# A list scheduler's costs and one new rule: two-tensor work of VectorE and GpSimd kept apart in an attention and feed-forward kernel

## The chip, the cores and the metric

The kernel runs on one core of a Trainium2 chip. Time is device time in microseconds (us) of one execution; for the kernel before it is 896.74 us, the median of three runs (894.29 to 896.76). The engines are called as the profile calls them: PE (TensorE, matmuls), DVE (VectorE), ACT (ScalarE), POOL (GpSimd) and SP, whose queue issues every DMA.

## The reference: what is computed

Attention with heads mixed before and after the softmax, then a feed-forward layer, cut to what matters:

```python
scores = scale * np.matmul(q, k.transpose(0, 1, 3, 2))        # 4 batches, 12 heads, 448 x 448, head width 64
scores = np.einsum('bhij,hg->bgij', scores, w_pre)            # heads mixed
scores = scores - np.max(scores, axis=-1, keepdims=True)
attn = np.exp(scores)
attn = attn / (np.sum(attn, axis=-1, keepdims=True) + 1e-09)
attn = np.einsum('bhij,hg->bgij', attn, w_post)               # heads mixed again
x = np.matmul(attn, v)                                        # then heads side by side: 1792 x 768
h = x @ w_in                                                  # 768 x 2048
g = h * (1.0 / (1.0 + np.exp(-1.702 * h)))
out = g @ w_out                                               # 2048 x 768
```

The weights of the feed-forward layer come as 64-bit floats, which the kernel converts by integer operations.

## The kernel before, in words

**Attention** goes in 180 steps, 45 for each of the 4 batches. A step takes 10 rows of all 12 heads, 120 partitions by 448 columns. The scores of a block of 112 rows are made on PE (`qk`), copied out of PSUM (`sc`), written to DRAM (`sd`) and gathered again in the layout of the steps (`r`). A step is then: mixing matmul `mx` (PE), negated maximum `nm` (DVE), exponential `e` with its row sum (ACT), `rs` (POOL adds a small number, DVE takes the reciprocal), weighting, second mixing `pp` (PE), and a copy `p` out of PSUM. In the first two batches ("whole", f32) POOL scales the small mixing matrix (`wr`). In the last two ("half") everything is split into an upper and a lower f16 part: `a1` on ACT, `w` and the lower part `a2 = w - a1` on POOL, and a lower part of `p` on DVE. Every 12 steps a product `av` with v makes a piece of `x`.

**Weights** are converted in 16 pieces (`w0_s` for w_in, `w1_s` for w_out, s from 0 to 7), each in three thirds: a load, `magnitude` on ACT, then four operations on DVE (`least`, `shift`, `rest` at L542, `sign` at L548) in place on `w_f`, a sum of squares on ACT, one small matmul `sums` (L113) that adds over the partitions, `scale_w` on DVE, an upper part on ACT (L576), a lower part `w_p` on DVE (L581), and a store `wd` to DRAM. Whoever needs the piece loads it again (`wt`).

**Feed-forward** goes in 32 units (8 slices of 256 of the 2048 columns, for each of the 4 batches): two groups of 18 matmuls `h` (L612), a tanh and a gate (`th`), the two parts of `g` (L637 ACT, L641 DVE), and six groups of six matmuls `po` (L650). A group is collected into `acc` either by one operation on DVE (L674) or by ACT into `pt` (L672) and an addition on POOL (L678).

**The order.** Nothing of this order is written out. Every operation is a task in a list scheduler (`add`, `run_all`): a task has an engine or a choice of two, `occ` (how long it holds its engine), `lat` (when its result can be used), a due time, and buffers that it takes. `run_all` keeps a clock for each engine, looks at the tasks that could start first on each, takes the most due of those within 0.1 us, and emits its instruction. So the figures set the order of each engine's queue, and nothing else: on the chip each engine works through its queue in that order and waits for semaphores where a value is not there yet. A number that is wrong by a tenth moves many rows a little.

Tile names below have the step, unit or piece in them: `nm_76` is the maximum of step 76, `h_7_0` the first half of unit 7, `w1_7_p` the converted piece 7 of w_out.

## Time and profile before

| | |
|---|---|
| median of 3 runs | 896.74 us (894.29 to 896.76) |
| the profiled execution | 895.33 us, of which 893.6 us are its span |
| PE busy | 856.5 us, 96% of the span |
| DVE, ACT, POOL busy | 631.0 (71%), 626.7 (70%), 353.3 (40%) |
| granted PE clock, mean | 0.99 of full speed |
| DMA | 196.85 MB, mean 220 GB/s |

The span is the time from the first to the last instruction; the rest of the execution's time lies around it. Shares over the whole span mix stages: the first 175 us are attention with transfers and conversions, from 178 us feed-forward work fills PE as well, the conversions end at about 401 us, and the last batch's feed-forward fills the time from about 750 us to the end. A wait on PE is idle time in front of an instruction, with the instruction that ended last among those it waited for.

### The profile page before, as it was taken

The page shows a single profiled execution, that of the slowest core. Times are in us where ns is not written, and L with a number is a line of the kernel's source. Part 1 is how long each engine was busy: PE and PEld are TensorE (multiplying, and loading weights), DVE is VectorE, ACT ScalarE, POOL GpSimd, SP SyncE. Part 2 cuts the span into 40 slices and gives each one's busy share as a digit, 9 for nine tenths or more (in the row PEclk, how much of TensorE's full clock was granted, in tenths as well). Part 3 has the DMA queues.
Part 4 walks back from the last instruction along what each step waited for, and adds up shares of the span by engine and source line. Part 5 has one row for each costly group of instructions (what it writes and reads, how often), then busy time and mean ns, then how long its engine had stood idle before and what let it go on. Part 6 is the DMA issues. An engine that isn't in the chain of part 4 may idle for free.

```text
span 893.6 us, 19386 instructions
## 1 busy us (share of the span) xinstructions
PE 856.5 (96%) x7030; PEld 541.5 (61%) x7030; DVE 631.0 (71%) x1471; ACT 626.7 (70%) x1389; POOL 353.3 (40%) x542
## 2 busy tenths in 40 slices
PE   8879998999998999889999999999999999999998
PEld 4546766566665666655666666665666666555554
DVE  3658769887879989999679877778675754342233
ACT  4769888987976888866788778776776675324442
POOL 0212222221217423565446745555355554204432
PEclk9989999999999999999999999999999999999999
DMA  8999999899987886789588495567563423352422
GB/s 248 303 300 325 293 329 311 294 322 316 321 313 256 295 268 209 242 213 299 171 275 236 145 287 170 164 183 236 173 187 103 156 73 114 108 163 101 142 76 93
DMA packets 66768, 196.85 MB, mean 220 GB/s; under 512 B 8081, under 2 KB 32913, under 8 KB 66673
## 3 DMA queue, kind: packets, MB, share of 16 engines
q1 hardware_dynamic: 66672, 195.62, 68.0%
q8 instruction: 55, 0.90, 0.4%
q14 instruction: 41, 0.33, 0.1%
HBM read 138.96 MB, written 56.62 MB: 219 GB/s over the span
## 4 chain that ended last, share of the span: by engine, by line
PE 60%; DVE 17%; DMA 10%; ACT 7%; issue 3%; POOL 2%; SPq 1%; ACTq 0%; POOLq 0%; DVEq 0%
PE po L650 18%; PE h L612 18%; PE pp L373 4%; PE mx L322 4%; PE av L460 3%; DVE nm L332 2%; PE av L449 2%; DMA sd<-sc 2%; DVE sc L278 2%; PE qk L252 2%; ACT e L342 2%; DVE w_f L542 2%; DVE w_f L548 2%; DMA w<-in_moe_w_in_dram 1%; DVE w_p L581 1%
## 5 line engine op out<-in xcount | busy, mean ns | idle before, releaser
L612 PE MATMUL h<-x,wt 128*128 128x448 f16 x1152 | 246.2, 353 | 1.5 <-ACT e L342 1.1
L650 PE MATMUL po<-g,wt 128*128 128x448 f16 x1152 | 238.9, 353 | 2.2 <-DVE th L631 1.1
L612 PEld LDWEIGHTS <-wt 128*128 128x128 f16 x1152 | 110.3, 98 | 102.4 <-issue 12.2
L650 PEld LDWEIGHTS <-wt 128*128 128x128 f16 x1152 | 110.0, 98 | 98.1 <-issue 3.1
L353 POOL TENSOR_SCALAR rs<-sm 120x1 f32<-120x1 f32 x180 | 46.3, 257 | 277.6 <-ACT e L342 272.2
L332 DVE TENSOR_REDUCE nm<-mx 120x1 f32<-120x448 f32 x180 | 110.1, 617 | 27.6 <-PE mx L322 13.7
L678 POOL TENSOR_TENSOR acc<-acc,pt 128x448 f32<-128x448 f32 x71 | 83.4, 1175 | 110.2 <-ACT pt L672 102.9
L396 POOL TENSOR_TENSOR a<-w,a 120x448 f16<-120x448 f32 (+1 forms) x90 | 97.9, 1088 | 28.9 <-issue 12.7
L373 PEld LDWEIGHTS pp<-wr,e 120*112 120x112 f32 x720 | 85.6, 178 | 35.9 <-issue 18.4
L631 DVE SCALAR_TENSOR_TENSOR th<-th,h 128x448 f32<-128x448 f32 x64 | 39.5, 618 | 82.7 <-ACT th L627 82.1
L373 PE MATMUL pp<-wr,e 120*112 120x120 f32 x720 | 91.7, 271 | 5.9 <-POOL wr L363 5.8
L322 PE MATMUL mx<-r,wa 120*120 120x448 f32 x180 | 84.7, 561 | 10.8 <-DMA r<-sd 9.3
L342 ACT ACTIVATE e<-mx,nm,c 120x448 f32<-120x448 f32 (+1 forms) x90 | 65.3, 726 | 27.6 <-DVE nm L334 17.5
L382 POOL TENSOR_SCALAR w<-e,rs 120x448 f32<-120x448 f32 (+1 forms) x90 | 61.5, 683 | 54.7 <-DVE rs L358 34.1
L674 DVE SCALAR_TENSOR_TENSOR acc<-po,ct,acc 128x448 f32<-128x448 f32 x97 | 65.5, 678 | 15.7 <-PE po L650 15.3
L390 ACT ACTIVATE a<-e,rs 120x448 f16<-120x448 f32 (+1 forms) x90 | 60.0, 667 | 23.6 <-DVE rs L358 21.8
L672 ACT ACTIVATE pt<-po,ct 128x448 f32<-128x448 f32 x71 | 44.9, 636 | 42.9 <-PE po L650 42.9
L342 ACT ACTIVATE e<-mx,nm 120x448 f32<-120x448 f32 (+1 forms) x90 | 57.7, 641 | 19.3 <-DVE nm L332 15.3
L363 POOL TENSOR_SCALAR wr<-wp,rs 120x120 f32<-120x120 f32 (+1 forms) x90 | 46.0, 512 | 58.0 <-DVE rs L358 41.3
L435 DVE TENSOR_TENSOR p<-pp,p 112x480 f16<-112x480 f32 (+1 forms) x90 | 58.2, 649 | 14.9 <-ACT p L431 14.3
L411 PE MATMUL pp<-wp,a 120*112 120x120 f16 x360 | 62.5, 217 | 0.7 <-POOL a L396 0.7
L409 PE MATMUL pp<-wp,a 120*112 120x120 f16 x360 | 62.6, 217 | 0.0
(141 smaller groups left out, 1568.6 us busy)
## 6 DMA issues: line engine op xcount, KB each, us to landing
wt<-wd SPq DMA_DIRECT2D x64, 768.0 KB, 4.3
sd<-sc SPq DMA_DIRECT2D x90, 392.0 KB, 4.7
r<-sd SPq DMA_DIRECT2D x164, 210.0 KB, 4.8
w<-in_moe_w_in_dram SPq DMA_DIRECT2D x24, 512.0 KB, 6.1
w<-in_moe_w_out_dram SPq DMA_DIRECT2D x24, 512.0 KB, 4.9
wd<-w_p SPq DMA_DIRECT2D x16, 768.0 KB, 5.8
out_dram<-acc SPq DMA_DIRECT2D x24, 224.0 KB, 4.9
kf<-in_k_dram SPq DMA_DIRECT2D x6, 448.0 KB
```

The costliest lines, as they stand in the source:

```text
L322: nc.tensor.matmul(mx[:K, :S], st["wa"][:K, :K], r[:K, :], start=True, stop=True)
L332: nc.vector.tensor_reduce(nm[:K], row["mx", i][:K, :S], axis=AX.X, op=ALU.max, negate=True)
L342: nc.scalar.activation(e[:K], row.pop(("mx", i))[:K, :S], AF.Exp, bias=row.pop(("nm", i))[:K, 0:1], scale=1.0 if b < WHOLE else st["c", b] ...
L373: nc.tensor.matmul(pp[:CP, jc * K:(jc + 1) * K], e[:K, jc * CP:(jc + 1) * CP], wr[:K, :, :n], start=True, stop=True,)
L382: nc.gpsimd.tensor_scalar(w[:K], e[:K], row["rs", i][:K, 0:1], 1.0, op0=ALU.mult, op1=ALU.mult)
L396: nc.gpsimd.tensor_tensor(a2[:K], row.pop(("w", i))[:K], row["a1", i][:K], op=ALU.subtract)
L409: nc.tensor.matmul(o, a1[:K, js], wp1[:K, :, :n], start=True, stop=False)
L411: nc.tensor.matmul(o, a2[:K, js], wp1[:K, :, :n], start=False, stop=True)
L612: nc.tensor.matmul(h, w[:, i, c, fc * 128:(fc + 1) * 128], x[:, j, c, :], start=(n == 0), stop=(n == len(terms) - 1),)
L650: nc.tensor.matmul(po, w[:, j, fc, e * 128:(e + 1) * 128], g[:, i, fc, :], start=(n == 0), stop=(n == len(terms) - 1),)
L674: nc.vector.scalar_tensor_tensor(a, po, c, a, op0=ALU.mult, op1=ALU.add)
L678: nc.gpsimd.tensor_tensor(a, a, st.pop(("pt", u, e)), op=ALU.add)
```

## The change

Four edits, all in the figures and rules of the scheduler; no instruction's work changes.

1. A rule: tasks marked `kind="two"` (operations that read two tensors from SBUF) on DVE ("D") and on POOL ("G") may not overlap in the plan. Marked are, on DVE, the lower parts of the inputs (L224), `rest` and `sign` of the conversion, its lower part (L581) and the lower part of `g` (L641); on POOL, `a2` (L396) and the addition into `acc` (L678).
2. The small matmul of a sum (`sums`) may start in the plan only 1.0 us after its last input is there.
3. The maximum is planned with 0.64 us (first two batches) and 0.77 us (last two) in place of 0.53 and 0.73.
4. The exponential is planned with 0.61 and 0.71 us in place of 0.62.

```diff
+    free_port = [0.0]
...
+                    if j["kind"] == "two" and e in "DG":
+                        s = max(s, free_port[0])
...
+            if j["kind"] == "two" and e in "DG":
+                free_port[0] = s + occ
...
-        j = add("PE", 0.12, over, list(after), due, 0.4, takes=[("gen", h)])
+        after = [add("-", 0.0, lambda: None, list(after), due, 1.0)]
+        j = add("PE", 0.12, over, after, due, 0.4, takes=[("gen", h)])
...
-        k = add("D", 0.73 if half else 0.53, lambda: peak(i), [m], i - 1, 0.81 if half else 0.62)
+        k = add("D", 0.77 if half else 0.64, lambda: peak(i), [m], i - 1, 0.86 if half else 0.73)
...
-            lo = add("G", 1.12, lambda: lower(i), [w, u], i + 0.6, 1.05, takes=[("a2", a2)])
+            lo = add("G", 1.12, lambda: lower(i), [w, u], i + 0.6, 1.05, takes=[("a2", a2)], kind="two")
...
-            low.append(add("D", 0.66, lambda a=a: c["w_lower"](a), [u], due + 0.5, 0.75))
+            low.append(add("D", 0.66, lambda a=a: c["w_lower"](a), [u], due + 0.5, 0.75, kind="two"))
```

What the new plan does with the rows: PE has the same instructions in another order, above all in the first 430 us of the span; after unit 11 its order differs in a handful of places. Seven collections of `po` go from ACT and POOL to DVE (L674 stands 104 times in place of 97, L678 64 times in place of 71). Three places follow.

DVE at step 76, around the lower parts of the weights' piece `w0_5`. Before:

```order
L631 SCALAR_TENSOR_TENSOR th_3_1_3500<-th_3_1_3500,h_3_1_3423 128x448
L581 SCALAR_TENSOR_TENSOR w0_5_p_3509<-w0_5_f0_3118,w0_5_s_3489,w0_5_p_3509 128x512
L581 SCALAR_TENSOR_TENSOR w0_5_p_3509<-w0_5_f1_3236,w0_5_s_3489,w0_5_p_3509 128x512
L581 SCALAR_TENSOR_TENSOR w0_5_p_3509<-w0_5_f2_3377,w0_5_s_3489,w0_5_p_3509 128x512
L641 SCALAR_TENSOR_TENSOR g_3_3335<-th_3_1_3500,gs_90,g_3_3335 128x448
L332 TENSOR_REDUCE nm_76_3547<-mx_76_3496 120x1
L224 SCALAR_TENSOR_TENSOR kp0_2_3498<-kb0_2_3415,s_k2_3217,kp0_2_3498 128x896
L332 TENSOR_REDUCE nm_77_3571<-mx_77_3541 120x1
```

And now:

```order
L117 TENSOR_REDUCE w0_5_n_3509<-sums_15_3496 128x1
L332 TENSOR_REDUCE nm_76_3518<-mx_76_3487 120x1
L85 TENSOR_SCALAR w0_5_n_3509<-w0_5_n_3509 128x1
L86 TENSOR_SCALAR ew_89<-w0_5_n_3509 128x1
L562 TENSOR_SCALAR ew_89<-ew_89 128x1
L564 RECIPROCAL w0_5_s_3526<-ew_89 128x1
L565 TENSOR_SCALAR w0_5_s_3526<-w0_5_s_3526 128x1
L641 SCALAR_TENSOR_TENSOR g_3_3302<-th_3_1_3490,gs_90,g_3_3302 128x448
L224 SCALAR_TENSOR_TENSOR kp0_2_3494<-kb0_2_3428,s_k2_3239,kp0_2_3494 128x896
L581 SCALAR_TENSOR_TENSOR w0_5_p_3544<-w0_5_f0_3162,w0_5_s_3526,w0_5_p_3544 128x512
L581 SCALAR_TENSOR_TENSOR w0_5_p_3544<-w0_5_f1_3245,w0_5_s_3526,w0_5_p_3544 128x512
L581 SCALAR_TENSOR_TENSOR w0_5_p_3544<-w0_5_f2_3379,w0_5_s_3526,w0_5_p_3544 128x512
```

The maximum `nm_76` stood behind three lower parts `w0_5_p` and the lower part of `g_3`; now it stands ahead of them, and the second sum of a piece (`w0_5_n`) directly ahead of it.

PE at the sum of the last weight piece, `w1_7` (`h_7_1` is unit 7's hidden layer, `po_6_5` unit 6's last output group, `qk_2_2_3` scores). Before:

```order
L612 LDWEIGHTS wt0_7_4954
L612 MATMUL h_7_1_5088<-x_0_742,wt0_7_4954 128x448
L113 MATMUL sums_22_5161<-w1_7_m_4585,ones_77 128x3
L650 LDWEIGHTS wt1_6_4673
L650 MATMUL po_6_5_5163<-g_6_4478,wt1_6_4673 128x448
```

And now:

```order
L262 MATMUL qk_2_2_3_0_5213<-kp1_2_3521,qp1_2_3717 112x448
L262 LDWEIGHTS qp1_2_3717
L262 MATMUL qk_2_2_3_1_5214<-kp1_2_3521,qp1_2_3717 112x448
L113 MATMUL sums_22_5227<-w1_7_m_4497,ones_77 128x3
L612 LDWEIGHTS wt0_8_5066
```

The sum stood behind `h_7_1` and ahead of `po_6_5`; now `po_6_5` (6 matmuls), `mx_100` (3), `pp_97` (12 short ones) and the scores `qk_2_2_2` and `qk_2_2_3` (12) are issued ahead of it.

DVE at the end of that piece's conversion (`w1_7_p`), and then the queue of SP from its store `wd1_7` to the load `wt1_7`, which the output groups of unit 7 need. DVE before:

```order
L581 SCALAR_TENSOR_TENSOR w1_7_p_5207<-w1_7_f0_4730,w1_7_s_5181,w1_7_p_5207 128x512
L581 SCALAR_TENSOR_TENSOR w1_7_p_5207<-w1_7_f1_4748,w1_7_s_5181,w1_7_p_5207 128x512
L641 SCALAR_TENSOR_TENSOR g_7_5185<-th_7_1_5170,gs_90,g_7_5185 128x448
L581 SCALAR_TENSOR_TENSOR w1_7_p_5207<-w1_7_f2_4911,w1_7_s_5181,w1_7_p_5207 128x512
L332 TENSOR_REDUCE nm_100_5256<-mx_100_5187 120x1
L334 TENSOR_SCALAR nm_100_5256<-nm_100_5256,c_2_3417 120x1
L674 SCALAR_TENSOR_TENSOR acc_0_2595<-po_6_5_5163,ct_6_4401,acc_0_2595 128x448
```

DVE now:

```order
L657 TENSOR_TENSOR ct_7_5126<-eo_91,ew_89 128x1
L620 TENSOR_SCALAR ct_8_5288<-ex_79,ew_89 128x1
L278 SCALAR_TENSOR_TENSOR sc_2_2_2_5224<-qk_2_2_2_1_5204,sc_2_2_2_5224 112x448
L278 SCALAR_TENSOR_TENSOR sc_2_2_3_5238<-qk_2_2_3_0_5213,sc_2_2_3_5238 112x448
L581 SCALAR_TENSOR_TENSOR w1_7_p_5270<-w1_7_f0_4563,w1_7_s_5254,w1_7_p_5270 128x512
L581 SCALAR_TENSOR_TENSOR w1_7_p_5270<-w1_7_f1_4717,w1_7_s_5254,w1_7_p_5270 128x512
L581 SCALAR_TENSOR_TENSOR w1_7_p_5270<-w1_7_f2_4933,w1_7_s_5254,w1_7_p_5270 128x512
L631 SCALAR_TENSOR_TENSOR th_8_0_5308<-th_8_0_5308,h_8_0_5230 128x448
```

SP before:

```order
L587 DMA wd1_7_124<-w1_7_p_5207 128x3072
L288 DMA sd_2_2_103<-sc_2_2_2_5234 112x1792
L309 DMA r_105_5299<-sd_2_1_102 120x896
L309 DMA r_106_5323<-sd_2_1_102 120x896
L288 DMA sd_2_2_103<-sc_2_2_3_5244 112x1792
L309 DMA r_107_5347<-sd_2_1_102 120x896
L600 DMA wt1_7_5362<-wd1_7_124 128x3072
```

SP now:

```order
L587 DMA wd1_7_124<-w1_7_p_5270 128x3072
L309 DMA r_107_5347<-sd_2_1_102 120x896
L288 DMA sd_2_2_103<-sc_2_2_3_5238 112x1792
L309 DMA r_108_5380<-sd_2_1_102 120x896
L309 DMA r_109_5407<-sd_2_1_102 120x896
L600 DMA wt1_7_5425<-wd1_7_124 128x3072
```

On DVE the last of `w1_7_p` now stands behind `nm_100` with its factor, the collection of `po_6_5`, a lower part `p` and three `sc`, all of which followed it before. On SP the gathers `r_108` and `r_109` now stand ahead of `wt1_7`. On PE `po_7_0` itself moves behind 12 matmuls of `h_9_0` and one `pp`.

## Rows read from the trace of the kernel before

**Rows 1.** The page: busy time, share of the span, count of each engine.

```profile
PE 856.5 (96%) x7030; PEld 541.5 (61%) x7030; DVE 631.0 (71%) x1471; ACT 626.7 (70%) x1389; POOL 353.3 (40%) x542
```

**Rows 2.** Stretches: length, busy of PE, PEld, DVE, ACT, POOL; clock, DMA, GB/s.

```profile
50.00:75.00 25.00, 21.95 (x178) 15.48 (x179) 16.70 (x45) 17.46 (x45) 5.26 (x16) 0.88 0.89 294
145.00:175.00 30.00, 26.84 (x216) 17.41 (x215) 26.61 (x73) 26.25 (x66) 7.55 (x19) 0.94 0.92 309
260.00:415.00 155.00, 144.04 (x1083) 92.15 (x1078) 146.51 (x325) 121.52 (x273) 78.74 (x96) 0.98 0.80 252
415.00:880.00 465.00, 460.51 (x4174) 284.51 (x4173) 286.93 (x645) 296.56 (x610) 214.74 (x287) 1.00 0.52 165
```

**Rows 3.** Waits of PE, whole span: total us, times, longest.

```profile
PE pp L373 <- POOL wr L363: 5.8, 6, 2.3
PE sums L113 <- ACT waste L100: 4.0, 4, 2.3
PE av L449 <- DVE p L435: 2.2, 1, 2.2
PE mx L322 <- DMA r<-sd: 9.3, 5, 5.2
```

**Rows 4.** Timeline of PE: start, us, instruction; idle before it and its releaser.

```profile
154.61 1.38 PE L373 MATMUL pp<-wr,e 120*112 120x120 f32 x8 [1.38 <-POOL wr L363]
281.49 1.94 PE L373 MATMUL pp<-wr,e 120*112 120x120 f32 x8 [2.31 <-POOL wr L363]
371.70 2.04 PE L449 MATMUL av<-p,vf 112*64 112x88 f32 x48 [2.22 <-DVE p L435]
392.91 0.39 PE L113 MATMUL sums<-w_m,ones 128*128 128x3 f32 x2 [2.33 <-ACT waste L100]
414.43 5.85 PE L650 MATMUL po<-g,wt 128*128 128x448 f16 x30 [0.99 <-DMA wt<-wd]
```

**Rows 5.** DVE by line, 60 to 260 us: count, busy us, mean ns, idle before.

```profile
L581 DVE SCALAR_TENSOR_TENSOR w_p<-w_f,w_s,w_p 128x512 f16<-128x512 f32 x27 | 19.2, 751 | 0.4 <-ACT w_p L576 0.2
L536 DVE TENSOR_SCALAR w_f<-w_f 128x512 int32<-128x512 int32 x28 | 12.3, 444 | 0.3
L641 DVE SCALAR_TENSOR_TENSOR g<-th,gs,g 128x448 f16<-128x448 f32 x7 | 4.8, 680 | 0.1
```

**Rows 6.** DVE by line, 260 to 415 us, as rows 5.

```profile
L278 DVE SCALAR_TENSOR_TENSOR sc<-qk,sc 112x448 f16<-112x448 f32 x34 | 19.8, 617 | 0.5 <-ACT sc L274 0.4
L581 DVE SCALAR_TENSOR_TENSOR w_p<-w_f,w_s,w_p 128x512 f16<-128x512 f32 x18 | 16.1, 937 | 0.4 <-ACT w_p L576 0.3
L674 DVE SCALAR_TENSOR_TENSOR acc<-po,ct,acc 128x448 f32<-128x448 f32 x16 | 10.8, 676 | 0.3 <-PE po L650 0.3
L536 DVE TENSOR_SCALAR w_f<-w_f 128x512 int32<-128x512 int32 x16 | 9.7, 613 | 0.0
L641 DVE SCALAR_TENSOR_TENSOR g<-th,gs,g 128x448 f16<-128x448 f32 x11 | 9.1, 827 | 1.3 <-ACT g L637 1.3
```

**Rows 7.** Timeline of DVE at two places between 275 and 391 us.

```profile
275.34 1.55 DVE L641 SCALAR_TENSOR_TENSOR g<-th,gs,g 128x448 f16<-128x448 f32 x1
...
384.76 1.65 DVE L542 SCALAR_TENSOR_TENSOR w_f<-w,w_f 128x512 int32<-128x512 int32 x1
...
386.79 0.91 DVE L542 SCALAR_TENSOR_TENSOR w_f<-w,w_f 128x512 int32<-128x512 int32 x1
...
389.67 1.61 DVE L548 SCALAR_TENSOR_TENSOR w_f<-w,w_f 128x512 int32<-128x512 int32 x1
```

**Rows 8.** Timeline of POOL beside rows 7, from 384.7 us.

```profile
384.72 1.13 POOL L678 TENSOR_TENSOR acc<-acc,pt 128x448 f32<-128x448 f32 x1
385.83 1.33 POOL L382 TENSOR_SCALAR w<-e,rs 120x448 f32<-120x448 f32 x1
```

**Rows 9.** Timeline of the DMA queue of SP: the store of the last converted weights.

```profile
400.70 0.34 SPq L587 DMA_DIRECT2D wd<-w_p  x1
```

**Rows 10.** The chain that ended last: the load that PE waits for at 414.43.

```profile
405.90 8.48 DMA wt<-wd
```

More of the change, by code (lines that the diff above doesn't have):

```diff
@@ L936, in step_tasks @@
             m["from"] = READY[i]
-        k = add("D", 0.73 if half else 0.53, lambda: peak(i), [m], i - 1, 0.81 if half else 0.62)
+        k = add("D", 0.77 if half else 0.64, lambda: peak(i), [m], i - 1, 0.86 if half else 0.73)
         early = expos.get(i, {"then": []})["then"]
-        e = expos[i] = add("A", 0.62, lambda: expo(i), [k, expos.get(i - 1)], i - 0.8, 0.73, takes=[("e", e_home[i])])
+        e = expos[i] = add("A", 0.71 if half else 0.61, lambda: expo(i), [k, expos.get(i - 1)], i - 0.8, 0.82 if half else 0.73, takes=[("e", e_home[i])])
         e["then"] += early
@@ L1063, in split_tasks @@
                     [j, sized[name, b]], x + 2 + i, {"G": 1.05, "A": 1.05}, takes=[(f"{name}p{i}", in_home[name, b, i])], bias=0.5)
-            lo = add("D", 1.65 if name == "v" else 1.05, lambda i=i: lower_part(name, b, i), [u], x + 2.5 + i)
+            lo = add("D", 1.65 if name == "v" else 1.05, lambda i=i: lower_part(name, b, i), [u], x + 2.5 + i, kind="two")
             h += [u, lo]
@@ L1077, in conversion_tasks @@
             for n, (name, occ) in enumerate((("magnitude", 0.62), ("least", 0.35), ("shift", 0.35), ("rest", 0.61), ("sign", 0.61))):
-                j = add("D" if n else "A", occ, lambda a=a, name=name: c[name](a), [j], due, occ + 0.09, takes=[] if n else [("wf", wf)])
+                j = add("D" if n else "A", occ, lambda a=a, name=name: c[name](a), [j], due, occ + 0.09, takes=[] if n else [("wf", wf)],
+                        kind="two" if n > 2 else "")
                 w64.append(j)
@@ L1202, in attention_then_feed_forward @@
             up = add("A", 0.56, lambda u=u, fc=fc: g_upper(u, fc), [d] + lower_g[:1], due + 1, 0.67, takes=[] if fc else [("g", g_home)])
-            lo = add("D", 0.6, lambda u=u, fc=fc: g_lower(u, fc), [up], due + 1.2, 0.7)
+            lo = add("D", 0.6, lambda u=u, fc=fc: g_lower(u, fc), [up], due + 1.2, 0.7, kind="two")
             th += [d, up, lo]
@@ L1230, in finish @@
                     collect_rest(u, e)
-            k["rest"] = rests[u, e] = add("G", 1.2, finish, [j2], due + 1, 1.15)
+            k["rest"] = rests[u, e] = add("G", 1.2, finish, [j2], due + 1, 1.15, kind="two")
             gen.append(j2)
```

## The prediction, made before the changed kernel was run

> **What bounds the kernel now.** First the page's busy shares: PE is busy 96% of the span [rows 1], so nearly all of the 893.6 us is PE's own work, whose instructions the change leaves as they are. What can move is PE's idle time, 37 us in all (893.6 less 856.5), and time at a lower granted clock. Next the busy time by stretches [rows 2]: from 415 to 880 us PE idles 4.5 us in 465, with DVE at 287; from 260 to 415 us it idles 11.0 us in 155, and there DVE is busy for 146.5 of 155. So that stretch is where the order of DVE reaches PE. Last the waits of PE one by one [rows 3, 4]. Three large ones lie in it: 2.31 us at 281.49 for a `wr` of POOL, 2.22 at 371.70 for a `p` of DVE, 2.33 at 392.91 for a sum of squares on ACT. The fourth, 0.99 at 414.43, is a load of converted weights. The largest wait of the whole span, 5.2 us for a gather [rows 3], lies at 47 to 53 us, in front of where the order changes much; it stays.
>
> Why is DVE late? Its two-tensor operations stretch: `w_p` takes 751 ns on average up to 260 us and 937 after, `g` 680 and 827 [rows 5, 6]. Single cases show the cause: at 384.76 `w_f` takes 1.65 us while POOL's two-tensor addition runs from 384.72 for 1.13 [rows 7, 8], that is, the rest of POOL's instruction and then its own time. There are eight such cases of two-tensor operations on both engines, the first at 275.34 and the last at 389.67 [rows 7], each 0.76 to 0.96 us longer than undisturbed, 6.9 us together. Two of the three large waits come right behind them: the three thirds of `w1_7` lose 2.7 us between 384 and 391, and the sum that PE waits for at 392.91 is theirs; a `w_p` just ahead of the `p` of 371.70 lost 0.9.
>
> **The change part by part.**
>
> *The sum of `w1_7`.* PE now has `po_6_5`, `mx_100`, `pp_97` and two pairs of scores ahead of it. Nine full matmuls among these are 9 x 0.195 = 1.8 us (5.85 us for 30 [rows 4]); the 24 short or paired ones bring it over 2.33, by an estimate from their count. The wait goes: -2.3. If DVE is later by as much, it stays: 0. I take -2.3, since DVE's four remaining operations on that piece no longer stand beside the busiest POOL stretch in the plan.
>
> *Step 76.* `nm_76` no longer stands behind three `w_p` and a `g`, so its exponential, `rs` and `wr` come earlier by more than the 2.31 us that PE waited. Bounds 0 and -2.3; I take -2.3, because the order alone does it, whatever collides.
>
> *The wait at 371.70.* `av_1_3_3` now follows two more pairs of scores, and the lower parts `w0_7_p` stand behind two `p`. Bounds 0 and -2.2, taken at half, -1.1: a collision there is still possible.
>
> *Early, at 154.61.* The `pp` that waited 1.38 us [rows 4] now follows two pairs of f32 scores. That stretch is also fed by transfers (share 0.92 [rows 2]), which can take it back: 0 to -1.4, half, -0.7.
>
> *The clock.* Over 260 to 415 us the granted clock averages 0.98, which is 3.1 us of full-speed work lost, and over 145 to 175 us 0.94 [rows 2]; the drops follow the large waits. Without two or three of these some returns: 0 to -3.1, taken at -0.9, since a new wait (next item) can bring a drop of its own.
>
> *The last conversion, later.* This speaks against the change. Ahead of the last `w1_7_p` on DVE now stand seven full operations more (a maximum, a `p`, three `sc`, the collection of `po_6_5`, and one collection more than before in the units ahead). At 0.58 (19.8 us for 34 [rows 6]) to 0.68 us each that is 4.1 to 4.7, say 4.4. The store was issued at 400.70 and the load `wt1_7` at 405.90, landing 8.48 later, when PE had waited 0.99 [rows 4, 9, 10]. On SP two gathers more stand ahead of the load, 0.34 each by the price of an issue [rows 9], 0.7. Against it, DVE loses less to collisions, up to 6.9, and `po_7_0` stands behind 12 matmuls more, 2.3 us of work that PE does while it waits. So the wait of 0.99 changes by 4.4 + 0.7 - 2.3 = +2.8 if no collision goes, and, as the three waits taken away bring PE there sooner, the load can cost up to +5.1. With half the collisions gone (3.5) and PE sooner, I take +2.0. Behind the waiting `po_7_0` on PE queue the other output groups of unit 7, `mx_106` and `pp_103`; their readers on DVE and ACT are then late too.
>
> *The rest.* The figures for maximum and exponential change no instruction. Seven collections more on DVE are 7 x 0.68 = 4.7 us [rows 6]; most lie where DVE has room (287 of 465 us [rows 2]); the cover is gone only in 260 to 415 us, where the one extra is counted above. The small reorderings up to 260 us and the other 27 sums, whose other waits are 1.7 us together [rows 3]: 0, with bounds -1.5 and +2.
>
> Sum: -2.3 -2.3 -1.1 -0.7 -0.9 +2.0 = -5.3. The profiled execution took 895.33 us (span 893.6 and 1.7 around it), 1.4 under the median. 895.33 - 5.3 = **890.0**.
>
> **A rule of the Trainium skill that speaks against it.** The trace shows DVE stretched by POOL operations with one tensor input as well: at 386.79 a `w_f` takes 0.91 us beside the one-input `w` of 385.83, which itself takes 1.33 [rows 7, 8]; and DVE's own one-input L536 goes from 444 to 613 ns [rows 5, 6], 16 x 0.17 = 2.7 us that the new rule does not look at. The Trainium skill, "SBUF — State Buffer", section "Who interferes with whom", says that a VectorE instruction with two SBUF inputs contends with any GpSimd instruction that reads SBUF, and that one-input VectorE operations contend too in their two-port modes. By that rule, with which these rows agree, keeping only two-tensor pairs apart moves collisions rather than removing them; that is the second case below.
>
> **The cases.**
>
> 1. *Forecast*: the order takes the waits at 281 and 393 away, part of the collisions go, the load `wt1_7` gives 2 us back. 890.0, its own range 887 to 893.5. Chance 0.46.
>
> 2. *The rule does not do what it says on the chip.* The plan's clocks and the chip's differ by more than the 0.7 us that an operation takes, and POOL's `w`, `rs` and input parts are not covered, so `w_f` and `w_p` meet other POOL work and about 6.9 us of stretching stays, at other places. Then the waits at 371.70 and 281.49 turn up elsewhere; only the sum's 2.3 goes and the load takes 2.0 of it: 895.33 - 2.3 + 2.0 = 895.0. For it: the eight cases, which nothing kept from meeting anywhere, are few among the marked DVE rows of the stretch (18 of L581 and 11 of L641 alone [rows 6]), so meeting is mostly chance. Against: `nm_76` and the sum move by order alone. Chance 0.23.
>
> 3. *All of it comes.* Everything PE waits for in 260 to 415 us except the load goes (11.0 - 1.0 = 10.0) with the clock's 3.1: 895.33 - 13.1 = 882. For it: most of these waits stand right behind a collision. Against: DVE stays at about 140 of 155 us there, and any full queue makes waits. Chance 0.13.
>
> 4. *Slower: the load of `wt1_7` becomes the wait.* If the collisions stay and DVE's seven operations are added, the load lands 5.1 us later against 2.3 us of work put ahead: +2.8 in the end. A wait of about 5 us also costs clock: after the one of 5.2 us, the stretch 50 to 75 us ran at 0.88 [rows 2, 3], 3.0 us lost. 895.33 + 2.8 + 3.0 = 901.1. It decides as soon as the load lands more than 2.3 us after 414.43 less whatever PE gained before. For it: DVE has hardly any idle time there. Against: some collisions have to go, by the moved rows alone. Chance 0.18.
>
> **How the numbers follow.** A difference of 0.3% (2.7 us) is about what a measurement of this kernel tells from none. Faster by more (under 894.05): cases 1 and 3, 0.59; within it: case 2, 0.23; slower by more (over 899.4): case 4, 0.18. The range from 883 to 900.5 takes in the bounds of the sum's terms; it leaves out the lower part of case 3 and the upper of case 4, under 0.2.
>
> **What will show it.** In the profile after: PE's waits for `sums` near none, and no wait over 1 us at steps 75 to 80; DVE's means for L581 and L641 between 260 and 415 us back toward 0.75 and 0.68; PE idle in that stretch near 6 us in place of 11.0. The load of `wt1_7` should be the longest wait of PE there, 2 to 4 us; over 5 is case 4, under 1 favours case 3. L536 stays near 0.6 us. Means of L581 and L641 that stay at 0.94 and 0.83 with fewer waits would mean that moved rows, not the rule, made the gain. I am wrong if new waits of PE arise before 260 us, or if the time changes by a drop of the clock at a place that these rows do not show.

## The result, and the profile after

The changed kernel takes 882.62 us (median of four runs, 879.38 to 884.72) against 895.82 us for the kernel before on the same chip (894.29 to 896.76). The ratio is 0.986, 95% interval 0.9831 to 0.9889: 13.2 us faster. The forecast was 890.0, with 887 to 893.5 as its own range; the direction was right, the gain was more than twice the 5.3 us of the sum. The nearest of the four cases is the third, "all of it comes" (882).

The profiled execution after took 879.38 us, the shortest of the four; so 15.9 us lie between the two traces, of which some 3 are scatter between runs. Where do they lie? A stretch cut by the clock on the wall holds different work in the two kernels. So the spans are cut where PE starts the same instruction in both: at the first matmul of unit 4 (`h_4_0`, 276.0 us before and 272.4 after) and at the first mixing matmul of step 110 (`mx_110`, 442.4 and 429.6). Stretches of the kernel before, columns as in [rows 2]:

```profile
0.00:276.00 276.00, 257.97 (x1837) 170.51 (x1838) 207.02 (x530) 218.24 (x532) 63.22 (x165) 0.98 0.92 302
276.00:442.40 166.40, 155.44 (x1285) 99.24 (x1284) 152.75 (x333) 124.99 (x278) 81.03 (x102) 0.98 0.78 247
442.40:893.60 451.20, 443.14 (x3915) 271.77 (x3912) 271.22 (x609) 283.42 (x580) 209.00 (x276) 1.00 0.51 160
```

The same three of the kernel after:

```profile
0.00:272.40 272.40, 255.80 (x1837) 169.56 (x1838) 206.69 (x531) 219.40 (x537) 65.45 (x165) 0.99 0.94 309
272.40:429.60 157.20, 150.42 (x1285) 97.42 (x1284) 146.04 (x334) 124.43 (x278) 80.86 (x101) 1.00 0.80 260
429.60:877.70 448.10, 443.10 (x3911) 271.38 (x3909) 274.46 (x615) 277.30 (x569) 205.77 (x270) 1.00 0.51 161
```

In the middle the same 1285 PE instructions take 5.0 us less (155.44 to 150.42) at a granted clock of 1.00 in place of 0.98, and PE idles 6.8 us in place of 11.0: -9.2 us. DVE needs 6.7 us less there for 334 instructions than before for 333. The first stretch gives -3.6 (busy -2.2, idle -1.4), the last -3.1, all of it idle time.

How much of the shorter busy time is the clock? Up to 60 us both kernels have one fall of it, from 49.4 us before and from 49.9 after. Behind that, while PE works, the granted clock of the kernel before falls from 1.00 to 0.50 (1.2 GHz) three times, each time at a wait of PE in [rows 4]: those of 1.38, 2.31 and 2.33 us. Three windows within these falls, columns as above:

```profile
155.30:158.60 3.30, 3.30 (x12) 1.48 (x10) 2.02 (x10) 3.05 (x9) 1.00 (x4) 0.50 0.98 395
281.60:284.90 3.30, 3.30 (x13) 2.33 (x14) 3.30 (x7) 1.91 (x5) 3.12 (x4) 0.50 1.02 356
394.20:397.50 3.30, 3.30 (x21) 2.41 (x21) 3.13 (x12) 2.78 (x6) 3.30 (x4) 0.50 0.71 194
```

Each takes about 1.7 us of full-speed work: 1.7 us in the first stretch and 3.4 in the middle. The changed kernel, without these waits, has none of the three. (Behind the wait of 2.22 us at 371.70 the clock did not fall.) So 5.1 us of PE's shorter busy time are clock in these two executions. That is a good draw: the clock over the whole span was 0.990 and 0.996 in them, but 0.992 in the other three runs of the changed kernel, and its mean over all runs is 0.9905 before (92 runs) and 0.993 after (4). By these means the clock is worth some 2 us (an estimate: 0.0025 of 885) of the 13.2, and the 0.004 by which the profiled execution stands out is about its 3 us under the median. For the span, the page's first line answers [rows 1]:

```profile
PE 849.3 (97%) x7030; PEld 538.3 (61%) x7030; DVE 627.2 (71%) x1478; ACT 621.1 (71%) x1382; POOL 352.1 (40%) x535
```

PE's 7030 instructions take 7.2 us less, the 5.1 of the clock and 2.1 that the clock does not account for; its idle time falls from 37.1 to 28.4 (8.7 us).

The largest waits of PE by kind, answering [rows 3] (total, times, longest):

```profile
PE mx L322 <- DMA r<-sd: 8.9, 5, 4.3
PE pp L373 <- POOL wr L363: 3.4, 4, 1.2
PE h L612 <- DVE th L631: 2.5, 2, 1.7
PE av L449 <- DVE sc L278: 1.6, 1, 1.6
...
```

Waits for `sums` (4.0 us before) are not among them nor in the rest of the list, and no output group of unit 7 waits for its load. PE's timeline shows what stands in place of the five of [rows 4], own times of the kernel after:

```profile
307.65 2.58 PE L449 MATMUL av<-p,vf 112*64 112x120 f32 x46 [1.62 <-DVE sc L278]
...
361.93 2.04 PE L449 MATMUL av<-p,vf 112*64 112x88 f32 x48 [0.71 <-DVE p L435]
...
374.26 6.04 PE L612 MATMUL h<-x,wt 128*128 128x448 f16 x31 [0.17 <-DMA wt<-wd]
...
381.81 1.34 PE L262 MATMUL qk<-kp,qp 64*112 64x448 f16 x12
383.15 0.39 PE L113 MATMUL sums<-w_m,ones 128*128 128x3 f32 x2
384.33 1.29 PE L612 MATMUL h<-x,wt 128*128 128x448 f16 x6 [0.79 <-DVE th L631]
...
393.43 1.30 PE L612 MATMUL h<-x,wt 128*128 128x448 f16 x6 [1.69 <-DVE th L631]
...
400.73 0.21 PE L409 MATMUL pp<-wp,a 120*112 120x120 f16 x1 [1.31 <-DVE th L631]
```

None is over 1.7 us, and all but the load's 0.17 end with DVE. The sum of `w1_7` (383.15) follows the scores without a wait. DVE by line over 260 to 415 us answers [rows 6]:

```profile
L278 DVE SCALAR_TENSOR_TENSOR sc<-qk,sc 112x448 f16<-112x448 f32 x36 | 20.8, 616 | 0.7 <-ACT sc L274 0.7
...
L674 DVE SCALAR_TENSOR_TENSOR acc<-po,ct,acc 128x448 f32<-128x448 f32 x23 | 15.4, 677 | 0.6 <-PE po L650 0.6
L581 DVE SCALAR_TENSOR_TENSOR w_p<-w_f,w_s,w_p 128x512 f16<-128x512 f32 x18 | 13.2, 783 | 0.6 <-ACT w_p L576 0.6
...
L536 DVE TENSOR_SCALAR w_f<-w_f 128x512 int32<-128x512 int32 x16 | 8.4, 543 | 0.0
...
L641 DVE SCALAR_TENSOR_TENSOR g<-th,gs,g 128x448 f16<-128x448 f32 x11 | 8.1, 739 | 0.7 <-ACT g L637 0.7
```

L581 falls from 937 to 783 ns, L641 from 827 to 739; L278 and L674, which read PSUM, stay at 616 and 677. DVE's timeline at the last conversion, and then SP's queue, answer [rows 7, 9]:

```profile
379.70 1.28 DVE L542 SCALAR_TENSOR_TENSOR w_f<-w,w_f 128x512 int32<-128x512 int32 x2
380.90 1.29 DVE L548 SCALAR_TENSOR_TENSOR w_f<-w,w_f 128x512 int32<-128x512 int32 x2
...
390.79 2.06 DVE L581 SCALAR_TENSOR_TENSOR w_p<-w_f,w_s,w_p 128x512 f16<-128x512 f32 x3
```

```profile
392.88 0.34 SPq L587 DMA_DIRECT2D wd<-w_p  x1
...
397.41 0.86 SPq L600 DMA_DIRECT2D wt<-wd  x2
```

These `rest` and `sign` operations of `w1_7` run undisturbed, two in 1.28 us where single ones took 1.65 and 1.61. The store goes out 7.8 us earlier (392.88 against 400.70). But PE starts `h_7_0` 9.3 us earlier (374.26 against 383.60), with `po_6_5` and `mx_100` already done; counted from `h_7_0` the store leaves 1.5 us later than before, and the load `wt1_7` is issued 0.8 us later (397.41). From issue to landing that load takes less than the 8.48 us of [rows 10]:

```profile
DMA to landing us min/median/max: 5.7/5.7/5.7
```

So it lands at 403.1, and PE comes to `po_7_0` at 404.7.

Below, "stretched time" is what DVE's two-tensor operations on `w_f`, `w_p`, `g` and the lower input parts take above their undisturbed durations (0.68 to 0.75, for the inputs 1.14 to 1.28 us), added over one trace: 16.1 us before, 6.4 after. The count depends on the durations taken as undisturbed: with slightly other ones single kernels move by up to 2 us, the means of groups of kernels by less than 1.

### The profile page after: what moved, and what is told of

It reads as the page before. It is cut to its first block, busy times and chain, and to the rows that moved or that the text cites. A ratio compares the mean times of both kernels' runs of the same rounds, so it can differ in the third digit from the quotient of the medians.

```text
span 877.7 us, 19384 instructions
## 1 busy us (share of the span) xinstructions
PE 849.3 (97%) x7030; PEld 538.3 (61%) x7030; DVE 627.2 (71%) x1478; ACT 621.1 (71%) x1382; POOL 352.1 (40%) x535
## 4 chain that ended last, share of the span: by engine, by line
PE 64%; DVE 15%; DMA 8%; ACT 6%; POOL 3%; issue 3%; SPq 1%; ACTq 0%; POOLq 0%; DVEq 0%
PE po L650 19%; PE h L612 18%; PE pp L373 5%; PE mx L322 5%; PE av L449 3%; DMA va<-in_v_dram 3%; PE qk L252 3%; PE av L460 3%; DVE nm L332 2%; DMA r<-sd 2%; DMA sd<-sc 1%; DVE w_p L581 1%; ACT waste L100 1%; DVE acc L674 1%; PE pp L409 1%
## 5 line engine op out<-in xcount | busy, mean ns | idle before, releaser
L353 POOL TENSOR_SCALAR rs<-sm 120x1 f32<-120x1 f32 x180 | 49.9, 277 | 282.9 <-ACT e L342 278.6
L678 POOL TENSOR_TENSOR acc<-acc,pt 128x448 f32<-128x448 f32 x64 | 74.6, 1168 | 106.6 <-ACT pt L672 99.5
L396 POOL TENSOR_TENSOR a<-w,a 120x448 f16<-120x448 f32 (+1 forms) x90 | 94.6, 1051 | 24.1 <-POOL w L382 8.4
L382 POOL TENSOR_SCALAR w<-e,rs 120x448 f32<-120x448 f32 (+1 forms) x90 | 68.7, 763 | 50.1 <-DVE rs L358 41.9
L674 DVE SCALAR_TENSOR_TENSOR acc<-po,ct,acc 128x448 f32<-128x448 f32 x104 | 70.1, 678 | 13.0 <-PE po L650 12.7
L672 ACT ACTIVATE pt<-po,ct 128x448 f32<-128x448 f32 x64 | 40.6, 636 | 46.0 <-PE po L650 45.6
L342 ACT ACTIVATE e<-mx,nm 120x448 f32<-120x448 f32 (+1 forms) x90 | 58.1, 646 | 15.9 <-DVE nm L332 12.3
L431 ACT CAST p<-pp 112x480 f16<-112x480 f32 (+1 forms) x90 | 50.1, 558 | 19.1 <-PE pp L411 18.7
L409 PE MATMUL pp<-wp,a 120*112 120x120 f16 x360 | 62.1, 216 | 1.3 <-DVE th L631 1.3
```

The costliest lines, as they stand in the source:

```text
L342: nc.scalar.activation(e[:K], row.pop(("mx", i))[:K, :S], AF.Exp, bias=row.pop(("nm", i))[:K, 0:1], scale=1.0 if b < WHOLE else st["c", b] ...
L382: nc.gpsimd.tensor_scalar(w[:K], e[:K], row["rs", i][:K, 0:1], 1.0, op0=ALU.mult, op1=ALU.mult)
L396: nc.gpsimd.tensor_tensor(a2[:K], row.pop(("w", i))[:K], row["a1", i][:K], op=ALU.subtract)
L409: nc.tensor.matmul(o, a1[:K, js], wp1[:K, :, :n], start=True, stop=False)
L674: nc.vector.scalar_tensor_tensor(a, po, c, a, op0=ALU.mult, op1=ALU.add)
L678: nc.gpsimd.tensor_tensor(a, a, st.pop(("pt", u, e)), op=ALU.add)
```

## The experiments

Theory 1: the rule makes the gain, by taking collisions away. Theory 2: the later product of the sums makes it. Theory 3: any new order moves the time by several us, and this is a good one. Theory 5, formed on the way: the three parts have a gain of their own together. (There is no theory 4.)

All kernels that the search orders anew (medians of 4 to 10 runs, stretched time from one profile each, the kernel before measured anew on the chip of each), with R for the rule, S for the later sums, T for the new figures; "nudge" is the planned duration of the mixing product, moved by 0.005 or 0.01 us, which means nothing on the chip but makes another order:

| kernel | parts | nudge | median us | ratio to before, 95% | stretched us |
|---|---|---|---|---|---|
| before | none | | 893.9 to 896.5 | 1 | 16.1 |
| before_nudged | none | +0.005 | 887.03 | 0.9933 (0.9914 to 0.9952) | 13.5 |
| before_nudged2 | none | +0.01 | 900.30 | 1.0048 (1.0013 to 1.0083) | 13.8 |
| before_nudged3 | none | -0.005 | 895.31 | 0.9983 (0.9962 to 1.0003) | 15.7 |
| rule_only | R | | 891.27 | 0.9971 (0.9955 to 0.9987) | 10.3 |
| rule_nudged | R | +0.005 | 889.22 | 0.9943 (0.9919 to 0.9968) | 11.8 |
| sums_only | S | | 895.24 | 1.0014 (0.9994 to 1.0034) | 16.5 |
| times_only | T | | 889.99 | 0.9968 (0.9934 to 1.0003) | 15.0 |
| no_rule | S, T | | 889.30 | 0.9941 (0.9918 to 0.9963) | 14.5 |
| no_rule_nudged | S, T | +0.005 | 889.63 | 0.9940 (0.9916 to 0.9964) | 16.4 |
| no_sums | R, T | | 892.34 | 0.9970 (0.9945 to 0.9995) | 9.3 |
| no_times | R, S | | 889.93 | 0.9939 (0.9919 to 0.9960) | 14.2 |
| after | R, S, T | | 882.62 | 0.9860 (0.9831 to 0.9889) | 6.4 |
| after_nudged | R, S, T | +0.005 | 882.32 | 0.9871 (0.9835 to 0.9908) | 8.8 |
| after_nudged2 | R, S, T | +0.01 | 887.03 | 0.9906 (0.9868 to 0.9943) | 6.6 |
| after_nudged3 | R, S, T | -0.005 | 886.94 | 0.9907 (0.9877 to 0.9937) | 12.4 |
| rule_wide | R wider, S, T | | 885.26 | 0.9878 (0.9847 to 0.9909) | 4.7 |

**One part alone.** Each kernel is the one before with one part of the diff:

```
rule_only:   free_port and kind="two", nothing else
sums_only:   after = [add("-", 0.0, lambda: None, list(after), due, 1.0)]
times_only:  0.73/0.53 -> 0.77/0.64 (maximum), 0.62 -> 0.71/0.61 (exponential)
```

> The rule that keeps marked two-tensor operations apart alone, with the old figures for maximum and exponential and the sums' product where it was. If the rule makes the gain (theory 1): about 885 us, stretched time of DVE's two-tensor operations falls from 16.1 us to about 6, PE's waits of 260 to 415 us fall from 11.0 to near 6. If the later product of the sums makes it (theory 2): 892 to 895, and the wait for a sum behind w1_7 (2.33 us) stays. If the order that the search falls upon decides, whatever the rule (theory 3): anything from 882 to 900, with no tie between the stretched time and the kernel's time.

> Only the product of the sums is placed 1 us later in the plan; no rule, old figures. Theory 1: within 2 us of 895.8, stretched time stays near 16 us. Theory 2: 885 to 889, PE's waits for sums (4.0 us) gone and the clock of 260 to 415 us up from 0.98 to 1.00. Theory 3: anything from 885 to 900.

> Only the planned durations of maximum and exponential at their traced values; no rule, product of the sums where it was. Theories 1 and 2: within 2 us of 895.8, with the stretched time near 16 us and the waits for sums near 4 us. Theory 3: away from 895.8 by 3 us or more in either direction, as the order is another one everywhere.

Measured: 891.27, 895.24 and 889.99. None comes near 885; theory 2's gain does not show. With the rule alone the stretched time falls to 10.3, not to theory 1's 6, and brings only 0.3% of the time. By the median the new planned durations alone do as much as the rule, though their interval (to 1.0003) takes in no gain at all.

**Another order and no part.** The control:

```
-    0.57 if half else 0.755, lambda: mix(i)
+    0.575 if half else 0.76, lambda: mix(i)
```

> Control: the kernel before with one planned duration moved by 0.005 us (the mixing product 0.755 to 0.76, its half 0.57 to 0.575), which has no meaning for the chip but makes the search fall upon another order. Theories 1 and 2: within 2 us of 895.8. Theory 3: 3 us or more away, in either direction, and this tells how much a new order alone is worth.

Measured: 887.03, ratio 0.9933. Half the change's gain, from a number without meaning. Theory 3 holds at least so far.

**All parts but one, and the nudge on the changed kernel.** The part is taken out of the changed kernel as it was put in above.

> The changed kernel without the rule; new figures and the later product stay. Theory 1 (the rule): 893 to 896, stretched time back near 15 us. Theory 3 (which order the search falls upon): anything from 882 to 900; the first four kernels lay at 887.0 to 895.2 with no tie to the stretched time (13.5 us at 887.0, 10.3 at 891.3).

> The changed kernel with the product of the sums back at its old place. Theory 1: 882 to 885. Theory 2 (the sums): 886 or more with waits for sums of 2 to 4 us and a clock of 0.98 in 260 to 415 us. Theory 3: anything from 882 to 900.

> The changed kernel with the old figures for maximum and exponential. Theory 1: 882 to 885. Theory 3: anything from 882 to 900.

> The changed kernel with the planned duration of the mixing product moved by 0.005 us, as in before_nudged. If all three parts together make a gain of their own (theory 1 or 2): within 2 us of 882.6. Theory 3: 3 us or more above 882.6, since that time would be one draw at the good end.

Measured: 889.30, 892.34, 889.93, each 7 to 10 us slower than the change, and after_nudged 882.32, as fast as it. Theory 1 alone misses all three: it asked for 893 to 896 without the rule and for 882 to 885 without either of the other parts. The kernel no_sums comes out as theory 2 had it (in its trace 4.3 us of waits for sums and a clock of 0.97 in 260 to 415 us), sums_only does not. after_nudged is against theory 3 in its plain form, and led to theory 5 and to more orders of both kernels (0.765/0.58 and 0.75/0.565 in the line above).

> The changed kernel with the mixing product planned 0.01 us longer (0.765, half 0.58): a third order with all three parts. If the three parts together have a gain of their own (theory 5, from the two equal times so far): 881 to 885. If 882.6 and 882.3 were both lucky (theory 3): 886 to 892, where the eight orders without all three parts lie (887.0 to 895.2, mean 890.6 apart from the kernel before).

> The changed kernel with the mixing product planned 0.005 us shorter (0.75, half 0.565): a fourth order with all three parts. Theory 5: 881 to 885. Theory 3: 886 to 892.

> The kernel before with the mixing product planned 0.01 us longer (0.765, half 0.58): a third order with none of the parts. Theory 5: 887 to 897, at least 4 us above the changed kernel with the same figure. Theory 3: 882 to 897, with no fixed distance to it.

> The kernel before with the mixing product planned 0.005 us shorter (0.75, half 0.565): a fourth order with none of the parts. Theory 5 (the three parts have a gain of their own, about 9 us on the mean): 887 to 900, so that the mean of the four stays near 894 against 884.7 of the four with all parts. Theory 3 (order alone): 882 to 900; under 884 would bring the two means within their spread.

Measured: 887.03 and 886.94 with all parts, 900.30 and 895.31 with none. One by one these come out as theory 3 had it: the first two lie in its 886 to 892 and outside theory 5's 881 to 885, and 900.30 lies above the 897 that both gave. What stands of theory 5 is the distance between the groups. The ratios of the four orders with all parts (0.9860 to 0.9907) and of the four with none (0.9933 to 1.0048) do not overlap; their means are 0.9886 and 0.9991, 9.4 us apart, with a standard error of 2.4 us from the spread of the orders. By the traces, whose spans differ by 10.7 us on the mean, 2.8 us lie ahead of `h_4_0`, where single orders of the two groups overlap, about 6 us between `h_4_0` and `mx_110` (157.2 to 161.6 us with all parts, 161.8 to 166.4 with none), and 1.9 behind it. Within a group the order alone is worth 4.2 us (all) to 10 us (none). So of the 12.5 us in the ratio 0.986, 9.4 belong to the parts on the mean, and 3.1 to the two orders that happen to be compared: the changed kernel's own is 2.3 better than the mean of its group, the old one's 0.8 worse.

The page's first line of before_nudged and then of before_nudged2, the two ends of that spread:

```profile
PE 853.9 (96%) x7030; PEld 539.2 (61%) x7030; DVE 622.6 (70%) x1464; ACT 628.1 (71%) x1397; POOL 346.7 (39%) x538
```

```profile
PE 862.0 (96%) x7030; PEld 544.2 (61%) x7030; DVE 629.2 (70%) x1471; ACT 627.3 (70%) x1391; POOL 341.6 (38%) x535
```

The same 7030 instructions of PE differ by 8.1 us, more than half of the 12.5 us between the spans (884.9 and 897.4). Idle time differs by 4.4 (31.0 and 35.4). The granted clock over the span was 0.992 in the one and 0.982 in the other. So a poor order pays for its waits twice, the second time in clock.

**The rule a second time, and without it.**

> The rule alone, in a second order (mixing product 0.76, half 0.575). Theory 1: 882 to 887. If the rule is worth a few us and the order as much: 886 to 893 (rule_only 891.3).

> All but the rule, in a second order (mixing product 0.76, half 0.575), the changed kernel's partner being after_nudged at 882.3. Theory 1: 890 to 896, stretched time near 14 us. Theory 3: 882 to 897.

Measured: 889.22 and 889.63. The rule alone is worth 5.1 us by its ratio (2.6 the first time), far from theory 1's 882 to 887; without the rule the time lies just under theory 1's 890. A fit of the first sixteen ratios of the table by the three parts as independent terms gives R -3.8, S -2.4 and T -3.1 us, each with a standard error of 1.6 to 1.8: no part is settled alone but perhaps the rule, and the three make up the 9.4.

**Fewer tensor reads on POOL, in an unchanged order.** Here nothing is ordered anew; `acc` and `a2` are formed in the same places, from one tensor; the second operand of these sums is left out. The edit, in the kernel before and in the changed one:

```
-  nc.gpsimd.tensor_tensor(a, a, st.pop(("pt", u, e)), op=ALU.add)
+  nc.gpsimd.tensor_scalar(a, st.pop(("pt", u, e)), 1.0, 1.0, op0=ALU.mult, op1=ALU.mult)
-  nc.gpsimd.tensor_tensor(a2[:K], row.pop(("w", i))[:K], row["a1", i][:K], op=ALU.subtract)
+  row.pop(("w", i))
+  nc.gpsimd.tensor_scalar(a2[:K], row["a1", i][:K], 1.0, 1.0, op0=ALU.mult, op1=ALU.mult)
```

> The order of the kernel before, instruction for instruction, but POOL's two additions over tensors (acc and a2) read one tensor in place of two; this leaves the second operand of these two sums out. So no two-tensor operation of POOL but those of the inputs meets one of DVE. Theory 1 (collisions of two-tensor operations cost the time): 885 to 889, stretched time from 16.1 us to 6 or less, PE's waits at 281, 372 and 393 us go or halve. Theory 3 (the order, not the collisions): within 3 us of 895.

> The order of the changed kernel, with POOL's two additions reading one tensor in place of two as in before_pool_one; the second operand of these sums is left out. Theory 1 (the gain is the collisions that went): there is little left to gain, 880 to 883, against -7 us in the order of before. If shorter POOL instructions are what gave before_pool_one its 7 us: as much again here, 875 to 877.

Measured: 887.72 (0.9922, 0.9896 to 0.9949) in the old order, 877.10 (0.9810, 0.9769 to 0.9850) in the new: -7.0 us and, from 0.9860, -4.5. The first fits theory 1's time but not its stretched time (9.3, not 6 or less); the second lies beside the 875 to 877 of shorter POOL instructions, not in theory 1's 880 to 883. PE's timeline of before_pool_one (its lines are numbered one higher from 396 on) at the three large waits of [rows 4] and behind them:

```profile
282.05 1.07 PE L373 MATMUL pp<-wr,e 120*112 120x120 f32 x8 [1.15 <-POOL wr L363]
...
368.15 2.04 PE L450 MATMUL av<-p,vf 112*64 112x88 f32 x48 [0.69 <-DVE p L436]
...
387.42 0.28 PE L113 MATMUL sums<-w_m,ones 128*128 128x3 f32 x2
...
396.95 0.35 PE L325 MATMUL mx<-r,wm 120*120 120x448 f16 x1 [1.70 <-DVE acc L675]
```

2.31 became 1.15, 2.22 became 0.69, and the wait for the sum, 2.33, is gone (387.42), with the order as it was; a wait of 1.70 for a collection by DVE comes behind it. So lighter work on POOL takes most of the three waits away with every engine's order as it was. Whether by fewer collisions or by being shorter, this test cannot part: the one-tensor forms take 608 and 618 ns on the mean where the two-tensor ones took 1175 and 1088. POOL's busy time in the page of before_pool_one, and then of after_pool_one:

```profile
PE 854.4 (96%) x7030; PEld 540.4 (61%) x7030; DVE 622.2 (70%) x1471; ACT 625.9 (71%) x1389; POOL 267.3 (30%) x542
```

```profile
PE 847.0 (97%) x7030; PEld 537.8 (62%) x7030; DVE 621.2 (71%) x1478; ACT 620.6 (71%) x1382; POOL 264.0 (30%) x535
```

POOL is 86 and 88 us shorter in the two, but stretched time falls by 6.8 us in the old order (16.1 to 9.3) and by 1.2 in the new (6.4 to 5.2). Taken as a price per us of stretched time and a fixed gain for shorter POOL work, 7.0 = 6.8c + p and 4.5 = 1.2c + p give c = 0.45 and p = 4.0. The intervals of the ratios are 2 to 4 us wide to each side, so c could as well be 0 or twice as much. Over the seventeen orders of the table the slope is 0.84 (standard error 0.23, correlation 0.69), most of it the distance between orders with and without the rule: among the eight without it there is no tie (0.09), among the nine with it the correlation is 0.57. By these two estimates the 9.7 us of stretched time that the change removed are worth 4.3 to 8.1 us. So theory 1 may be true in part; that collisions cost this much, apart from POOL's shorter work and from what else the three parts do to the order, is not shown.

**The sums alone, in an unchanged order.** Every other engine keeps its order; on PE each of the 28 products stands right ahead of its reader.

```
-            t["t"] = add_over(parts_of())
+            pass
-        k = add("D", 0.1, lambda: add_along(m(), t["t"]), [j], due, 0.18)
+        k = add("D", 0.1, lambda: add_along(m(), add_over(parts_of())), [j], due, 0.18)
```

> The order of the kernel before on every engine, but on PE each of the 28 products for sums stands right ahead of the instruction that reads it: the one of w1_7 behind the six matmuls of po_6_5. If the waits for sums are worth what they last (the prediction's first term): -2 to -4 us, 891 to 893, waits for sums (4.0 us) under 2. If PE only comes sooner to the next wait: within 1 us of 895.

Measured: 899.06, ratio 1.0056 (1.0034 to 1.0079): slower, which neither theory expected. PE's waits for sums did fall, from 4.0 to 1.8 us, but those for `wr` rose from 5.8 us to 9.9:

```profile
PE pp L373 <- POOL wr L363: 9.9, 8, 3.3
```

Its timeline at both:

```profile
285.94 1.79 PE L373 MATMUL pp<-wr,e 120*112 120x120 f32 x8 [3.35 <-POOL wr L363]
...
398.96 0.39 PE L113 MATMUL sums<-w_m,ones 128*128 128x3 f32 x2 [1.20 <-ACT waste L100]
...
402.96 3.56 PE L612 MATMUL h<-x,wt 128*128 128x448 f16 x18 [1.09 <-DVE th L631]
...
408.16 0.35 PE L325 MATMUL mx<-r,wm 120*120 120x448 f16 x1 [1.64 <-DVE acc L674]
```

The wait for the sum of `w1_7` falls from 2.33 to 1.20, but 1.09 and 1.64 come behind it, where [rows 4] had nothing. And DVE, at the same place:

```profile
390.80 1.65 DVE L542 SCALAR_TENSOR_TENSOR w_f<-w,w_f 128x512 int32<-128x512 int32 x1
392.83 0.92 DVE L542 SCALAR_TENSOR_TENSOR w_f<-w,w_f 128x512 int32<-128x512 int32 x1
```

These are the rows of the kernel before [rows 7], collisions and all (1.65 and 0.91 there), 6.04 us later. From `h_7_0` (383.6 and 389.7) to `po_7_0` (414.4 and 420.3) PE gains 0.2 us by the move. That fits DVE setting the pace there: PE spared one wait meets the next. The loss itself builds up further ahead, 3.4 us by `h_4_0` and 2.7 more by `h_7_0`, where the waits for `wr` grow; in between the one for `wr` at 285.94 is 3.35 us in place of 2.31. Why the moved products do that was not tried.

**A wider rule.** The changed kernel with two more operations of POOL under the rule:

```
-  w = add("G", 0.72, lambda: weigh(i), [v], i, 0.7, takes=[("e", w_home)])
+  w = add("G", 0.72, lambda: weigh(i), [v], i, 0.7, takes=[("e", w_home)], kind="two")
   (and kind="two" on the upper parts of the inputs)
```

> The changed kernel with the rule extended to POOL's one-tensor operations w and the upper parts of the inputs. If the rule was too narrow, as after_pool_one at 877.1 suggests: 877 to 881, stretched time under 5 us. If it is wide enough, or the wider one holds up DVE and POOL: 883 to 890.

Measured: 885.26 (0.9878, 0.9847 to 0.9909). Stretched time falls to 4.7, as asked, but the time lies within the spread of the four orders with all parts. It lies in the line on record for a rule that was wide enough already or holds up DVE and POOL (883 to 890). No version with all operands in place is clearly faster than the changed kernel.

## Why the prediction was right in direction and wrong in size

**The step that failed** is the one headed "the last conversion, later": +2.0 us, because DVE has seven operations more ahead of `w1_7_p` while PE comes to `po_7_0` sooner. The seven do stand there and PE does come sooner, but `po_7_0` waits for nothing: -1.0 in place of +2.0. The step held two things in their places that moved. DVE's queue came sooner together with PE: the store leaves 7.8 us earlier, and against PE only 1.5 us later, not far from the step's own 4.4 less 3.5. And the load, taken at 8.48 us from issue to landing, took 5.7; with 8.48 it would have come 1.2 us after PE. Why it took less was not tried.

The collisions of that piece did not go by half either; they moved. Its six `rest` and `sign` operations take 4.1 us after against 7.05 before (1.65, 0.91, 0.68, 1.52, 1.61, 0.68), the three `w1_7_p` 2.06 us without the 1.60 that one of them took: some 3.8 us of loss are gone. But its six operations with one input (L532 and L536), which lost 0.2 us before, lose 3.6 now; four of them stand in the rows of the last section. That is what the rule quoted in the prediction had said, for this piece; over the whole kernel the two-input loss falls by 9.7 us and the one-input loss stays (5.7 us before, 5.4 after).

**The clock** was mis-sized too, between these two executions by more than any other term: -0.9 for 260 to 415 us, bounded at -3.1 from a rounded 0.98. By the granted clock it was -3.4 there and -1.7 more at 155 us; over all runs it is some 2 us. The prediction had seen that the falls of the clock follow the large waits, and took the waits at 281.49 and 392.91 away, but of the falls behind these two, 1.7 us each, it gave back 0.9 us in all, since it expected a new one at the load.

Behind both stands that the sum priced waits one by one. In 276 to 442 us DVE is busy 152.75 of 166.4 us, in the kernel after nearly all that PE still waits for there ends with it, and its total, 6.7 us shorter after, had no term of its own.

**The other terms**, by the trace after:

| term | forecast | measured | why |
|---|---|---|---|
| sum of `w1_7` | -2.3 | -2.3 | by position, as forecast: `pp_97` and the scores fill PE up to 383.15, while the sum's inputs are there only 0.4 us sooner, counted from `h_7_0`; but a wait that goes is not a gain by itself: in before_sums_moved this one fell by 1.1 and PE gained 0.2 |
| step 76 | -2.3 | -2.3 | no wait there; fewer reads on POOL alone halved it (before_pool_one) |
| wait at 371.70 | -1.1 | -1.5 | 0.71 left at 361.93 |
| load `wt1_7` | +2.0 | -1.0 | as above |
| early | -0.7 | -3.6, 1.7 of it clock | before_nudged reached `h_4_0` at 272.8 with none of the parts, against 272.4: the draw of an order can give as much |
| PE's busy time, 276 to 442 us | -0.9 | -5.0, 3.4 of it clock | as above; 1.6 not explained |
| new or longer waits, 276 to 442 us | 0 | +2.9 | 1.62 at 307.65, 0.79 at 384.33, 1.69 at 393.43, 1.31 at 400.73, where the kernel before had less; each ends with DVE |
| after 442 us | 0 | -3.1 | the four orders with all parts take 447.8 to 448.8 us for it, the four with none 449.4 to 451.2: about 2 us of the change, not looked for, since little idle time stood there |

The measured column adds up to the 15.9 us between the two traces.

**The cases.** Case 2, that the rule does not do on the chip what it says, was half true: the nine orders with the rule have 4.7 to 14.2 us of stretched time (mean 9.4), the eight without it 13.5 to 16.5 (mean 15.2). It thins collisions out and forbids none: in the changed kernel a `g` at 385.29 still takes 1.34 us beside an input part of POOL that the rule does not mark. Case 4, a long wait for the load `wt1_7`, came in none of the traces: output groups wait at most 1.0 us for such a load. But loads of the other weights' pieces do hold up `h`, for 1.2 to 3.0 us in rule_only, no_times, no_rule_nudged and after_nudged. That the time lies at case 3's 882 is luck: that case had all of its 13.1 us between 260 and 415 us, and of the 15.9 us between the traces 9.2 lie in that part. What no case had is the largest thing found: that with nothing changed but the order, the time spreads from 887 to 900 us. A range for this change had to hold at least that.

## What to carry to other kernels

Where one engine is busy for nine tenths of a stretch, price a change there by what it does to that engine's total, and not by the waits of the engine that waits for it: those move on when one is taken away. Where a fall of TensorE's clock stands behind a wait, price the wait with it. Before giving a scheduler's rule the credit, run both kernels with a meaningless nudge in the planned figures, three or four times; here that alone was worth -6 to +4 us, and only the groups could be told apart. To test what collisions cost, keep the order and change what the instructions read.

## What the hardware showed beyond expectation

DVE's operations with one input collide too. In the changed kernel, DVE and then POOL:

```profile
370.88 0.42 DVE L532 TENSOR_SCALAR w_f<-w_f 128x512 f32<-128x512 f32 x1
372.18 1.22 DVE L532 TENSOR_SCALAR w_f<-w_f 128x512 f32<-128x512 f32 x1
374.70 2.40 DVE L536 TENSOR_SCALAR w_f<-w_f 128x512 int32<-128x512 int32 x2
```

```profile
372.08 1.04 POOL L396 TENSOR_TENSOR a<-w,a 120x448 f16<-120x448 f32 x1
...
374.50 1.03 POOL L396 TENSOR_TENSOR a<-w,a 120x448 f16<-120x448 f32 x1
375.50 1.32 POOL L678 TENSOR_TENSOR acc<-acc,pt 128x448 f32<-128x448 f32 x1
```

Undisturbed 0.42 us, beside POOL's additions 1.2: the one of 372.18, which started after POOL's instruction (372.08), ends 0.28 us after that has ended (373.12), so most of its 0.42 us of work came only then. In proportion (2.9 times) that is more than a two-tensor operation suffers (at most 2.4 times). All four DVE operations in these rows belong to `w1_7`. Over 260 to 415 us these two lines (L532, L536) lose 4.9 us before and 4.3 after (above the undisturbed 0.42), so the change left that loss where it was. The Trainium skill, "SBUF — State Buffer", section "Who interferes with whom", says that one-input operations in VectorE's two-port modes contend with GpSimd, and that the one issued second blocks fully. These rows agree as to which of the two waits; in which mode DVE ran, and whether it was blocked fully, no row tells. Over the seventeen orders such one-input loss has no tie to the time (correlation under 0.1, two-input between 0.7 and 0.8 in the same count), and why the one matters and the other not stays open.

On one chip, 23 runs of the kernel before lay between 891.90 and 899.96 us; the scatter within a kernel is nearly as large as the effect of one part, and a single profile can stand 7 us from the median (896.36 against 889.22 in rule_nudged), 3 us in the changed kernel.
